# The last stage's matmuls with all wide steps first, and the attention phase's result stores on ScalarE's queue

## The chip, the core and the metric

One core of a Trainium2 chip runs the whole program. The engines that matter are TensorE (PE, matmuls and their weight loads), VectorE (DVE), ScalarE (ACT) and SyncE (SP, which issues DMAs and computes nothing). Each runs its own list of instructions in order and waits on semaphores for the others. A DMA is put on a queue by the engine that issues it, SP or ACT, and is then carried out beside all else. The metric is the device time of one execution in microseconds, the median of the runs.

## What is computed

A memory attention over 8 batches, 8 heads, 576 positions and 64 dimensions, then two MLPs without residuals over the 4608 tokens, each with 512 model dimensions, 2048 hidden ones and a squared ReLU:

```python
a = softmax(phi, axis=2)                       # over 32 memories
k_m = einsum('bhsm,bhsd->bhmd', a, k);  v_m = einsum('bhsm,bhsd->bhmd', a, v)
attn = softmax(q @ k_m.T / 8)
x = (attn @ v_m)  -> (4608, 512)
x = (s * relu(x @ w_in) ** 2 + b) @ w_out      # moe
out = relu(x @ w_in2) ** 2 @ w_out2            # moe2
```

## The kernel before

Every product keeps single-precision accuracy by splitting each operand into a rounded high part and the rest (a "low" part), and adding three products (high x high, high x low, low x high). The last three products also use a scheme with 7 instead of 8 half-size products (`e` = 0 to 6), whose operands are sums and differences of quarter blocks.

There are four stages on TensorE. In the attention phase (lines 786 to 810) the attention is folded into the first layer's input weights: for each batch `b`, unit `f` of 128 hidden columns and half `half` of the 576 positions, `hidden` (line 582) runs 6 matmuls of 288 columns into one of three PSUM banks `hps`, and ACT evicts the bank with a ReLU into half of an SBUF tile `r` (line 593). A tile `r` (five of them) holds both halves, and after the second it is stored to the DRAM tensor `rd`, at line 803. There are 256 such halves and 128 stores. Between them, at slots given by tables, run all the other steps of the phase: transposes (`qps`, `pp`), scores (`sp`), sums (`kvs`), folds (`vps`, evicted by ACT and DVE into `vp`), exponentials, loads of the next batches, and near the end the combination of the first output weights (`wo`, `ws` into `w`) and the first squares and casts of the next stage.

The second stage multiplies the squared `r` by the first output weights (banks `ya`, `yb`, `yc`, 384 columns), the third by the second input weights (banks `pa`, `pb`, `pc`, 384 columns). The last stage (lines 1128 to 1143) takes 18 blocks of 256 tokens; for each of the 7 products of a block, `run` (line 1132) goes over the 8 units `u`. For each it runs one matmul of 512 columns, with the high part of the activations as the stationary operand against the high and low parts of the weights, and one of 256 columns, with the low part of the activations against the high part of the weights. All 16 add into one PSUM bank (`qa`, `qb` or `qc`, picked by `chain` at line 829), the 256-column ones into its first half.

The order of the instructions on ACT, DVE, PE and SP in the attention phase and in the last stage is that of the program text: the wrapper `Written` (line 163; lines 176 and 178 are where every such instruction is recorded) issues each one behind the one before on its engine. In the last stage, ACT's rounding casts (`hi`), DVE's subtractions that make the low parts (`lo`), ACT's evictions (`left`) and DVE's additions (`out`) stand in two lists that `go_on` walks through; before a product it goes on until that product's low part has been issued.

Of the kernel before, what the change touches and what calls it, by code (L numbers as in the profile page):

```python
# [89 lines left out]
def memory_attention_then_two_relu2_mlps(  # L90
# [36 lines left out]
    NU = NF // 2  # L127
# [18 lines left out]
    rd = [[dram.tile([P, NU, S], F32, name=f"rd{b}_{h}") for h in range(2)] for b in range(B)]  # L146
# [35 lines left out]
    pe, act, dve, sp = [Written(e) for e in (nc.tensor, nc.scalar, nc.vector, nc.sync)]  # L182
# [132 lines left out]
    def in_turn(jobs):  # L315
        for job in jobs:
            yield from job
# [52 lines left out]
    weight = lambda key, u, e: w2[key, u, e // 4][:, e % 4]  # L370
# [211 lines left out]
    def hidden(b, f, half, r):  # L582
        pt = at["pt", b]
        hps = ps_h.tile([P, 512], F32, tag="h", name="hps")
        t0 = half * HB
        i = 0
        for hp in range(2):
            w = at["vp", b, f // 4][:, hp, :, (f % 4) * P:(f % 4) * P + P]
            for wi, xi in split3:
                pe.matmul(hps[:, :HB], lhsT=w[:, wi], rhs=pt[xi][:, hp, t0:t0 + HB],  # L590
                                 start=(i == 0), stop=(i == 5))
                i += 1
        st["act"] = act.activation(r[:, t0:t0 + HB], hps[:, :HB], AF.Relu)
# [44 lines left out]
    def wo1_combos(u):  # L638
        tiles = unit_tiles(u)
        for i, t in enumerate(tiles):  # L640
            w2["one", u, i] = t.bitcast(F32R)
        yield from combos(of_out(wo1.pop(u)), lambda: w2["one", u, 0], lambda: w2["one", u, 1])
# [143 lines left out]
    for slot in range(SB * B):  # L786
        b, h = divmod(slot, SB)
        f, half = divmod(h, 2)
        if h == 0 and b == B - 2:
            kpart.close()  # L790
            wpools.append(ctx.enter_context(tc.tile_pool(name="wa", bufs=1)))
            turns.append((in_turn([wo1_combos(u) for u in range(NA)]), 1))
        for go, args in events.pop(slot, []):
            go(*args)
        if h == 0 and b == B - 1:
            lpart.close()
            wpools.append(ctx.enter_context(tc.tile_pool(name="wb", bufs=1)))
            turns.append((in_turn([wo1_combos(u) for u in range(NA, NU)]), 1))
        if half == 0:
            r = r_p.tile([P, S], F32, tag="r", name="r")  # L800
        hidden(b, f, half, r)
        if half == 1:
            sp.dma_start(rd[b][f // NU][:, f % NU], r)
        for turn in turns[:]:
            for _ in range(2):
                if next(turn[0], turns) is turns and turn in turns:
                    turns.remove(turn)
        for go, *args in [x for a, x in zip(BEGUN, BEGIN1) if a == slot]:
            dict(sq=square, cast=cast)[go](0, *args)
# [19 lines left out]
    def chain(e, banks, n, run, name):  # L829


        key = "acacaba"[e]
        start = e in (0, 1, 5)
        if start:
            banks[key] = bank(name + key)
        to = banks[key][:, :n]
        run(to, start)
        return to
# [24 lines left out]
    for n in range(NBLK1):  # L863
        banks, outs = {}, {}
        for e in range(7):
# [5 lines left out]
            start = e in (0, 1, 5)  # L871
            if start:
                banks[key] = [bank("y" + key)[:, :TP] for _ in range(2)]
            to = banks[key]
            for part in range(4):
                for go, *args in parts.pop(28 * n + 4 * e + part, []) + win.pop(28 * n + 4 * e + part, []):
                    go(*args)
                for d in range(2):
                    for u in range(UQ):
                        w = weight("one", part * UQ + u, e)  # L880
                        for i, (wi, xi) in enumerate(split3):
                            pe.matmul(to[d], lhsT=w[:, wi, d], rhs=cast1[n, e, part][:, u, xi],
                                             start=(start and part == 0 and u == 0 and i == 0),
                                             stop=(part == 3 and u == UQ - 1 and i == 2), skip_group_check=True)
# [49 lines left out]
    raws, casts, late = {}, {}, []  # L934
# [41 lines left out]
    for p in range(NPAIR):  # L976
        last = p == NPAIR - 1
        for u0 in range(0, NU, 2):
# [13 lines left out]
            for e in range(7):  # L992
                for u, banked, room in zip(units, banks, rooms):

                    def run(to, start):
                        w, xc = weight("in", u, e), xcs[p, e]
                        for n, (kk, (wi, xi)) in enumerate((kk, s) for kk in range(2) for s in split3):
                            pe.matmul(to, lhsT=w[:, wi, kk], rhs=xc[:, xi, kk],
                                             start=(start and n == 0), stop=(n == 5), skip_group_check=True)
                    to = chain(e, banked, TP, run, "p")  # L1000
                    c11, c12, c21, c22 = [room[:, i, j] for i in range(2) for j in range(2)]
                    out_ = (c11, c22, c12, c12, c22, c11, c21)[e]
                    if e < 3:
                        st["act"] = act.copy(out_, to)
                    elif e < 6:
                        add(out_, to, out_)
                        st["dve"] = dve.scalar_tensor_tensor(out=out_, in0=out_, scalar=0.0, in1=out_,
                                                                   op0=ALU.max, op1=ALU.mult)
                    else:
                        act.activation(out_, to, AF.Relu)  # L1010
                        st["act"] = act.activation(out_, out_, AF.Square)
                    if e > 4:
                        h = e - 5
                        late.append((gd[p][h][:, :, u, :],
                                     room[:, h].rearrange("p t c -> p (t c)").rearrange("p (n c) -> p n c", n=3)))
                        if not (last and u0 == NU - 2):
                            sp.dma_start(*late.pop())
# [104 lines left out]
    def go_on(until):  # L1122
        while not until():
            x = next(x for x in (his, todo) if x and can(*x[0])).pop(0)
            dict(hi=hi, lo=lo, less=less_, out=out_, left=left)[x[0]](*x[1:])
            made.add(x)

    for n in range(NBLK2):
        for e in range(7):
            go_on(lambda: ("lo", e, n) in made and (e not in (2, 3, 4, 6) or ("out", e - 2, n) in made))  # L1130

            def run(to, start):
                for u in range(NU):
                    w = weight("out", u, e).rearrange("p i k c -> p (i k c)")
                    pe.matmul(to, lhsT=casts[n, e](u, 0), rhs=w, start=(start and u == 0), stop=False, skip_group_check=True)
                    pe.matmul(to[:, :256], lhsT=casts[n, e](u, 1), rhs=w[:, :256], start=False, stop=(u == NU - 1),
                              skip_group_check=True)
            banks[n, e] = chain(e, banks, 512, run, "q")
            made.add(("pe", e, n))
            rooms.append(held.pop((n, e)))  # L1140
            if (n, e) == (0, 3):
                rooms += [(rc_turn[0] + i) % 4 for i in range(2)]
# [30 lines left out]
```

## Time and profile before

| what | value |
|---|---|
| median of 3 runs | 1426.86 us (1420.91 to 1429.13) |
| the profiled execution's own time | 1426.42 us |
| its span | 1424.6 us |
| PE busy with matmuls | 1390.2 us (98%) |
| DVE busy | 1118.8 us (79%) |
| ACT busy | 791.3 us (56%) |
| 128 stores `rd` from `r`, issued by SP | 288 KB each, 3.7 us to landing (median) |
| 70 stores of the output from SP, 2 from ACT | 128 KB each, 2.4 and 2.5 us to landing |

Busy times of different engines overlap. A matmul's duration contains its way through the array, so durations of neighbours overlap as well, and the time from one start to the next is what counts. DMA issues are not counted as busy time of an engine, though they hold its queue. Names like `r<-hps` say which tile is written from which; a line number 176 or 178 is that of the wrapper.

### The profile page before, as it was taken

What the parts mean: (1) busy time and instruction counts of PE and PEld (TensorE: products, weight loads), DVE (VectorE), ACT (ScalarE), POOL (GpSimd) and SP (SyncE); (2) the same over time, 40 slices, a digit from 0 to 9 for tenths busy, and PEclk for the clock granted to TensorE, in tenths of its full rate; (3) what the DMA queues carried; (4) which work ended last, traced back from release to release, by engine and by line L of the source; (5) the groups of instructions that cost most, each with busy time, mean ns of one, the idle gap of its engine ahead of it and who ended that gap; (6) DMA issues with size and microseconds to landing.
All of it is one profiled execution on the core that took longest, in us unless ns stands there. A gap on an engine that the chain in (4) does not pass through costs nothing.

```text
span 1424.6 us, 26004 instructions
## 1 busy us (share of the span) xinstructions
PE 1390.2 (98%) x10352; PEld 1293.3 (91%) x10352; DVE 1118.8 (79%) x1670; ACT 791.3 (56%) x1397; POOL 1.2 (0%) x8
## 2 busy tenths in 40 slices
PE   4899999999999999999999999999999999999998
PEld 3788888888999999999999999999998888888887
DVE  6766787676788989898759687686659888888886
ACT  3556666677776877767445455454444444444442
POOL 0000000000000000000000000000000000000000
PEclk9999999999999999999999999999999999999999
DMA  9979889536485674764995664756797434443341
GB/s 308 299 233 302 275 269 293 190 126 216 135 288 164 217 246 152 252 212 165 343 394 191 240 222 174 280 182 257 265 369 268 119 115 140 146 148 119 116 138 35
DMA packets 209160, 306.30 MB, mean 215 GB/s; under 512 B 48400, under 2 KB 163088, under 8 KB 201488
## 3 DMA queue, kind: packets, MB, share of 16 engines
q1 hardware_dynamic: 208880, 304.40, 63.5%
q8 instruction: 81, 1.33, 0.4%
q10 hardware_dynamic: 160, 0.26, 0.1%
q14 instruction: 39, 0.32, 0.1%
HBM read 180.88 MB, written 123.73 MB: 214 GB/s over the span
## 4 chain that ended last, share of the span: by engine, by line
PE 90%; DVE 4%; DMA 2%; ACT 2%; issue 1%; SPq 0%; ACTq 0%; DVEq 0%
PE ya L178 14%; PE qa L178 14%; PE pa L176 13%; PE hps L178 12%; PE yc L178 7%; PE qc L178 7%; PE pc L176 6%; PE yb L178 4%; PE qb L178 3%; PE pb L176 3%; PE vps L178 2%; PE sp L178 1%; DMA gd<-gr 1%; PE kvs L178 1%; PE qps L178 1%
## 5 line engine op out<-in xcount | busy, mean ns | idle before, releaser
L178 PEld LDWEIGHTS hps<-pt,vp 128*128 128x128 f32 x1536 | 210.2, 190 | 36.3 <-issue 18.1
L178 PE MATMUL hps<-pt,vp 128*128 128x288 f32 x1536 | 234.5, 304 | 4.8 <-ACT r L178 2.0
L178 PE MATMUL qa<-w,gc 128*128 128x512 f32 (+1 forms) x1152 | 212.6, 340 | 0.2 <-DVE o L178 0.2
L178 PE MATMUL ya<-rcast,w 128*128 128x384 f32 x1152 | 202.9, 336 | 0.8 <-ACT r L178 0.8
L178 PEld LDWEIGHTS qa<-w,gc 128*128 128x128 f32 x1152 | 176.5, 188 | 27.4 <-DVE o L178 0.5
L178 PEld LDWEIGHTS ya<-rcast,w 128*128 128x128 f32 x1152 | 199.9, 188 | 1.0 <-ACT r L178 1.0
L176 PE MATMUL pa<-xc,w 128*128 128x384 f32 x1056 | 195.3, 337 | 0.0
L176 PEld LDWEIGHTS pa<-xc,w 128*128 128x128 f32 x1056 | 184.5, 188 | 0.5
L178 DVE TENSOR_TENSOR gc<-h,gc 128x1024 fp32r<-128x1024 f32 (+1 forms) x137 | 145.0, 1080 | 23.3 <-ACT gc L178 23.3
L178 ACT CAST gc<-h 128x1024 fp32r<-128x1024 f32 (+1 forms) x137 | 125.1, 938 | 40.1 <-DVE h L178 36.2
L178 ACT ACTIVATE r<-hps 128x288 f32<-128x288 f32 x256 | 104.5, 417 | 66.8 <-PE hps L178 49.8
L178 PE MATMUL qc<-w,gc 128*128 128x512 f32 x576 | 107.7, 340 | 0.0
L178 DVE TENSOR_TENSOR rcast<-r,rcast 128x768 fp32r<-128x768 f32 x96 | 90.6, 954 | 20.9 <-ACT rcast L178 20.1
L178 PE MATMUL yc<-rcast,w 128*128 128x384 f32 x576 | 101.8, 336 | 0.0
L178 PEld LDWEIGHTS qc<-w,gc 128*128 128x128 f32 x576 | 88.2, 188 | 13.5
L178 PEld LDWEIGHTS yc<-rcast,w 128*128 128x128 f32 x576 | 100.0, 188 | 0.0
L176 PE MATMUL pc<-xc,w 128*128 128x384 f32 x528 | 99.6, 336 | 0.0
L178 ACT CAST rcast<-r 128x768 fp32r<-128x768 f32 x96 | 78.2, 834 | 37.9 <-DVE r L178 33.2
L178 ACT COPY o<-qa 128x256 f32<-128x256 f32 x54 | 20.1, 371 | 134.6 <-PE qa L178 134.6
L176 PEld LDWEIGHTS pc<-xc,w 128*128 128x128 f32 x528 | 92.5, 188 | 0.0
L178 DVE TENSOR_TENSOR rcast<-rz,rcast 128x768 fp32r<-128x768 f32 x72 | 68.1, 954 | 16.7 <-ACT rcast L178 16.1
L178 ACT CAST rcast<-rz 128x768 fp32r<-128x768 f32 x72 | 58.7, 836 | 37.8 <-DVE rz L178 24.4
(283 smaller groups left out, 1921.6 us busy)
## 6 DMA issues: line engine op xcount, KB each, us to landing
rd<-r SPq DMA_DIRECT2D x128, 288.0 KB, 3.7
gd<-gr SPq DMA_DIRECT2D x96, 384.0 KB, 3.8
h<-gd SPq DMA_DIRECT2D x34, 1024.0 KB, 4.9
wt<-in_moe_w_out_dram SPq DMA_DIRECT2D x16, 1024.0 KB, 6.6
r<-rd SPq DMA_DIRECT2D x16, 768.0 KB, 5.5
rz<-rd SPq DMA_DIRECT2D x16, 768.0 KB, 5.8
kv<-in_k_dram SPq DMA_DIRECT2D x24, 384.0 KB, 5.3
kv<-in_v_dram SPq DMA_DIRECT2D x24, 384.0 KB, 5.9
```

What stands on the lines that cost most here:

```text
L176: return go(*args, **kwargs)
L178: self.last = go(*args, **kwargs)
```

## The change

Line 803 issues the store of `r` on ACT's queue in place of SP's, right behind the second eviction that it carries away. In the last stage, `run` makes two loops of one: first the 8 matmuls of 512 columns, then the 8 of 256.

```diff
         hidden(b, f, half, r)
         if half == 1:
-            sp.dma_start(rd[b][f // NU][:, f % NU], r)
+            act.dma_start(rd[b][f // NU][:, f % NU], r)
...
             def run(to, start):
+                w = [weight("out", u, e).rearrange("p i k c -> p (i k c)") for u in range(NU)]
                 for u in range(NU):
-                    w = weight("out", u, e).rearrange("p i k c -> p (i k c)")
-                    pe.matmul(to, lhsT=casts[n, e](u, 0), rhs=w, start=(start and u == 0), stop=False, skip_group_check=True)
-                    pe.matmul(to[:, :256], lhsT=casts[n, e](u, 1), rhs=w[:, :256], start=False, stop=(u == NU - 1),
+                    pe.matmul(to, lhsT=casts[n, e](u, 0), rhs=w[u], start=(start and u == 0), stop=False, skip_group_check=True)
+                for u in range(NU):
+                    pe.matmul(to[:, :256], lhsT=casts[n, e](u, 1), rhs=w[u][:, :256], start=False, stop=(u == NU - 1),
                               skip_group_check=True)
             banks[n, e] = chain(e, banks, 512, run, "q")
```

## Rows read from the trace of the kernel before

**Rows 1.** The page's chain that ended last: share of the span by engine

```profile
PE 90%; DVE 4%; DMA 2%; ACT 2%; issue 1%; SPq 0%; ACTq 0%; DVEq 0%
```

**Rows 2.** Busy us by stage; last columns: granted clock, DMA share, GB/s

```profile
0.00:361.00 361.00, 332.26 (x4305) 285.10 (x4306) 258.65 (x463) 225.50 (x545) 1.21 (x8) 0.99 0.77 250
361.00:702.00 341.00, 341.00 (x1968) 341.00 (x1969) 300.70 (x359) 244.50 (x305) 0.00 (x0) 1.00 0.64 213
702.00:1061.00 359.00, 358.14 (x2054) 356.36 (x2052) 257.17 (x449) 169.77 (x329) 0.00 (x0) 1.00 0.71 257
1061.00:1424.00 363.00, 358.80 (x2028) 310.87 (x2028) 302.31 (x402) 151.53 (x219) 0.00 (x0) 1.00 0.44 140
```

The engines stand in the order PE, PEld, DVE, ACT, POOL, each with its count of instructions.

**Rows 3.** The page's groups: busy, mean ns of one | idle before, releaser

```profile
L178 PE MATMUL qa<-w,gc 128*128 128x512 f32 (+1 forms) x1152 | 212.6, 340 | 0.2 <-DVE o L178 0.2
```

**Rows 4.** Timeline (start, us, what): first product, a weight load; loads by form

```profile
1063.49 2.98 PE L178 MATMUL qa<-w,gc 128*128 128x512 f32 x16
...
1056.55 0.32 SPq L178 DMA_DIRECT2D w<-wod  x1
...
w<-wod SPq DMA_DIRECT2D x8, 1024.0 KB, 7.7
```

**Rows 5.** Chain in order of time (start, us, what), 384 and 288 columns

```profile
677.32 8.32 PE yc L178 x48
...
92.74 6.38 PE hps L178 x48
```

**Rows 6.** The same chain in the last stage: two products, one by one

```profile
1106.46 2.82 PE qc L178 x16
1109.28 2.83 PE qa L178 x16
```

**Rows 7.** Groups by form, PE, 1100 to 1424: 512 and 256 columns

```profile
L178 PE MATMUL qa<-w,gc 128*128 128x512 f32 x520 | 186.0, 399 | 0.0
L178 PE MATMUL qa<-w,gc 128*128 128x256 f32 x520 | 146.0, 281 | 0.0
```

**Rows 8.** Groups by form, PE, 361 to 1061: 384 columns

```profile
L178 PE MATMUL yc<-rcast,w 128*128 128x384 f32 x576 | 101.8, 336 | 0.0
```

**Rows 9.** Tile `wsp`: duration ns min/median/max, first and last start

```profile
L178 PEld LDWEIGHTS wsp<-ones,wacc x16: 187/192/192, 290.5 to 292.2; 128*128 128x128 f32 x16
```

**Rows 10.** Tensor `rd`, 40 to 361 us: issues of the stores, ns min/median/max

```profile
L178 SPq DMA_DIRECT2D rd<-r x127: 319/333/1609, 40.6 to 360.8; - x127
```

**Rows 11.** Timeline: an eviction on ACT and its store on SP's queue

```profile
343.48 0.41 ACT L178 ACTIVATE r<-hps 128x288 f32<-128x288 f32 x1
...
343.92 0.32 SPq L178 DMA_DIRECT2D rd<-r  x1
```

**Rows 12.** Timeline, ACT: two evictions back to back

```profile
355.77 0.71 ACT L178 ACTIVATE r<-hps 128x288 f32<-128x288 f32 x2
```

**Rows 13.** Busy us in the attention phase (columns as in rows 2)

```profile
40.00:200.00 160.00, 153.84 (x2282) 128.80 (x2281) 115.93 (x194) 96.00 (x234) 0.00 (x0) 1.00 0.86 272
200.00:331.00 131.00, 131.00 (x1536) 115.15 (x1535) 93.11 (x173) 88.06 (x218) 0.00 (x0) 1.00 0.63 207
331.00:346.00 15.00, 14.45 (x106) 13.89 (x105) 12.04 (x30) 11.81 (x33) 0.00 (x0) 1.00 0.80 264
346.00:361.00 15.00, 12.53 (x84) 11.03 (x83) 10.63 (x21) 14.42 (x32) 0.00 (x0) 1.00 0.61 208
```

**Rows 14.** Tensor `rd`, 331 to 346 and 346 to 361: the stores

```profile
L178 SPq DMA_DIRECT2D rd<-r x9: 319/328/1022, 330.8 to 345.4; - x9
...
L178 SPq DMA_DIRECT2D rd<-r x8: 319/320/455, 346.9 to 360.8; - x8
```

**Rows 15.** Waits, 331 to 361: us in total, times, longest

```profile
PE hps L178 <- ACT r L178: 2.0, 5, 0.9
ACT r L178 <- DMA rd<-r: 1.5, 1, 1.5
```

**Rows 16.** Waits, 40 to 331

```profile
PEld hps L178 <- ACT r L178: 6.7, 8, 0.8
```

**Rows 17.** Tensor `out_dram` from 1380 us on: issues on both queues

```profile
L178 SPq DMA_DIRECT2D out_dram<-o x8: 466/466/590, 1387.5 to 1421.1; - x8
L178 ACTq DMA_DIRECT2D out_dram<-o x2: 497/527/557, 1420.3 to 1421.1; - x2
```

## The prediction

> **What bounds the kernel now.** I read the chain that ended last first, then the busy time of each engine by stage, then single groups of matmuls. TensorE carries 90% of the chain [rows 1], and the table by stage shows the same four times over: the attention phase (0 to 361 us), the two products of the first layer's output (361 to 702), of the second layer's input (702 to 1061) and of its output (1061 to the end) keep PE busy for 332, 341, 358 and 359 us, at a granted clock of 0.99 to 1.00 [rows 2], which is the upper of its two levels, 2.4 GHz. So a change counts if it alters the time from one matmul to the next, or if it makes PE wait. The two edits are in stages with different second-place engines. In the last stage ScalarE (ACT) is busy for 152 of 363 us and nothing presses. In the attention phase ACT is busy for 226 of 361 us [rows 2], and at that phase's end it is already the bound (below).
>
> **The last stage: the order of the wide and the narrow matmuls.** The edit adds and removes no instruction. A product has 8 matmuls of 512 columns and 8 of 256, and there are 18 blocks of 7 products, 126 in all. Before, they alternate; after, 8 wide ones run and then 8 narrow ones. Waits are no source of gain here: PE stood idle for 0.2 us before all 1152 matmuls into the bank `qa` [rows 3]. The new order needs the low halves (`lo`, VectorE) only half a product later, which relaxes a wait that costs nothing now. In the very first product it needs the last weight tile sooner: the eighth wide matmul starts after seven wide ones, not seven pairs. That product starts at 1063.49, and the tile's load is the first part of unit 7, on the queue at 1056.55 with some 7.7 us to landing [rows 4], so at about 1064.3. The new need is at 1063.49 + 7 x 0.227 = 1065.1, so I cost this at nothing; if the load lands as late as others do, it is under 1 us, once.
>
> What remains is the cadence. 48 matmuls of 384 columns take 8.32 us and 48 of 288 columns 6.38 us [rows 5], that is 173.3 and 132.9 ns each. At 2.4 GHz the columns alone are 160 and 120 ns, so a matmul with a weight load of its own costs 13 ns over its columns (13.3 and 12.9), at both widths. A product of the last stage takes 2.825 us [rows 6], or 353 ns for a pair, where columns and twice 13.3 ns make 213.3 + 106.7 + 26.7 = 346.7. Some 6.6 ns of a pair is thus unexplained, 126 x 8 x 6.6 = 6.7 us of the stage. Whether the new order gives it back depends on whose it is. If the narrow matmul's slot is 126.7 ns, because the weights of the next matmul cannot be loaded faster, then eight narrow slots cost the same wherever they stand: change zero. If it comes from changing width at each step, seven of eight such pairs vanish: -5.9 us. From above, a narrow matmul can hardly be slower than the 133 ns of the wider 288: 8 x 6.3 ns more for a product, +6.4 us. From below, 120 ns: -6.7 us.
>
> I take zero, by the mean durations. A 384-column matmul lasts 336 ns, 176 over its columns [rows 8]; a narrow one 281, 174 over them; a wide one 399, 186 over them [rows 7]. The extra 10 ns sits on the matmul that follows a narrow one and whose weights loaded meanwhile. That looks like a wait for weights, which the new order moves and doesn't remove. Against it: 16 weight loads beside two-column matmuls started within 1.7 us, about 113 ns apart [rows 9], so a load alone would fit under 120 ns. I leave that side a fair chance. The Trainium skill (TensorE: Matmul & The Clock Gate, LDWEIGHTS) puts a weight load at its columns over 1.2 GHz, 107 ns for 128, and (Back-to-back issue gap) a matmul at its columns over 2.4 GHz plus 2.5 ns. By both a pair would be 325 ns in either order and the edit would do nothing; the trace's 353 ns shows that the page misses 28 ns of a pair, so it can't decide between the two readings.
>
> **The attention phase: 128 stores move from SP's queue to ACT's.** Each tile `r` is filled by two ACT evictions and then stored. SP issues the store for about 0.33 us (319 to 1609 ns) [rows 10]. It starts right when the second eviction is done: an eviction from 343.48 for 0.41 us, its store at 343.92 [rows 11], 0.03 us later. On ACT the store stands behind that eviction in program order and must wait until its result is written. Everything queued behind it on ACT (the next evictions, casts of `pt` and `vp`, exponentials, the weight casts) waits as well, and PE waits for those through the three `hps` banks.
>
> The price of one store: ACT runs two evictions of 0.41 us in 0.71 [rows 12], so behind an eviction the next instruction starts after 0.30 us. After the change it starts after 0.41 + 0.03 + 0.33 + restart. The trace has no ACT instruction behind a DMA that ACT issued, so the restart is bounded: from 0.04 to 0.15 us, about one to five times the 0.03 us from eviction to store; I take 0.08, the low middle. That is 0.85 - 0.30 = 0.55 us a store.
>
> Where it lands: up to 331 us ACT has room, 64.0 us idle in 40 to 200 and 42.9 in 200 to 331 [rows 13]. 110 stores there would take 60 of 107 us. PE's own weight loads waited for evictions 8 times there, 6.7 us [rows 16]. If each of these spots got one store later, that is 8 x 0.55 = 4.4 us; if none, zero. I take 1.5, nearer to none, since in most of the stretch ACT waits for PE. In 331 to 361 it is different. Here ACT also does casts of weights and the first squares and casts of the next stage, and PE already waits for evictions five times [rows 15]. There are 8 stores in each half from 331 on (17 with the one at 330.8) [rows 14]. ACT's idle time is 15 - 11.81 = 3.2 us in the first half and 15 - 14.42 = 0.6 us in the second [rows 13]. The stores add 8 x 0.55 = 4.4 us to each, so 1.2 and 3.8 us come out over the room, 5.0 us, on the path, since the next stage's first matmul waits for ACT. Together +6.5 us. Low end: 0.50 us a store (4.0 us a half) gives 4.2, less 1.5 us for a wait of ACT for a free `r` tile [rows 15] that an earlier store would shorten: +2.7. High end: ACT's own two stores at the end took 0.53 us each where SP's took 0.47 [rows 17]; with 0.53 and the long restart a store costs 0.82 us, 9.4 at the end and up to 6.6 before: +16.
>
> On SP the 128 stores vanish, with every wait for an eviction in front of the loads behind them. That is worth nothing that I can find: none of the longer waits of PE between 40 and 361 us is for a load, while those for ACT are there [rows 15, 16]. The skill (DMA: Bandwidth & Descriptors, Issuing engines are not separate DMA queues) says that all issuers share the same 16 DMA engines and a second one saves only sequencer time; here it saves SP's, which isn't short, and spends ACT's.
>
> **The sum.** The profiled run took 1426.42 us with a span of 1424.6, beside a median of 1426.86, so it stands for the median within 0.5. 1426.4 + 6.5 + 0 = 1432.9, on the median 1433, +0.4%. A measurement of this kernel can tell about 0.5%, 7.1 us, so this is just inside no change.
>
> **Rivals.**
> Width changes are what costs the 6.6 ns: the last stage gives back 5.9 us and covers the stores, 1427. For it: the 113 ns of loads alone. Against: the 10 ns on the wide ones. Chance 0.28.
> Slower: ACT's queue is held longer than SP's issue shows, by long issues (up to 1609 ns here when DMAs are many [rows 10]) or by a store that waits for an earlier load's semaphore. The place is the whole phase; it decides when a store costs ACT over 107 / 110 = 0.97 us on average before 331, since then ACT is the bound throughout. Already at the high end, 0.82, it is 1426.4 + 16 = 1442; by two thirds of that, 1437 to 1442. Against: the usual issue is 0.33. The skill (Perfetto Trace Analysis, DMA Instruction, HWDGE) has an issue wait for a lock on a shared descriptor generator; with SP and ACT both issuing that would lengthen the store, in this direction. The trace has one such pair, an issue of SP and one of ACT that both began at 1421.1, and neither lasted longer than its queue's others [rows 17], so I give the lock little weight. Chance 0.17.
> The stores cost little, since ACT's end of phase has give that I don't see (the evictions can be late by three banks): 1426.4 + 2.7 or less, 1427 to 1429, and with the first rival 1421. Chance 0.08.
> Narrow after narrow is slower: 1432.9 + 6.4 = 1439. Chance 0.05.
> My own forecast, 1430 to 1436: 0.42.
>
> **How the numbers follow.** Slower by over 0.5% means above 1434.0: the second and fourth rival, and over a third of my own case: 0.17 + 0.05 + 0.16 = 0.38. Faster means below 1419.7, only with both gains at their best: 0.06. The rest, 0.56, is no change. The range is 1423 to 1441: below, the first rival with cheap stores; above, the slower rival short of its end.
>
> **What will show it.** In the last stage: 16 matmuls take 2.825 us (zero), 2.78 (width changes) or 2.88. In the attention phase: DMA issues on ACT, 128 of them, an ACT instruction 0.45 us or so behind each eviction's end, and more matmuls of `hps` that wait for `r` between 331 and the first `ya`, which moves from 360.9 to about 367. If that first `ya` starts before 364, or PE waits are spread from 100 us on, my account of ACT's room is wrong.

## The result and the profile after

| | before | after |
|---|---|---|
| median (range), us, 7 runs each | 1429.01 (1420.91 to 1429.41) | 1435.24 (1432.88 to 1436.26) |
| profiled execution, us | 1426.42 | 1435.44 |
| its span, us | 1424.6 | 1433.6 |
| first matmul of the second stage (`ya`) | 360.88 | 371.99 |
| first matmul of the last stage (`qa`) | 1063.49 | 1074.95 |
| from there to the end of the span | 361.11 | 358.65 |

The ratio is 1.006 with an interval of 1.0043 to 1.0077: slower, with 0.5% inside the interval. Against the 1433.0 that was forecast the median is 2.2 us higher. The table shows that this near hit is made of two misses of opposite sign. The attention phase lost 11.1 us where 6.5 was forecast, the two stages in the middle 0.35, and the last stage gained 2.5 where nothing was forecast: 11.1 + 0.35 - 2.5 = 9.0, the difference of the spans.

The page's chain that ended last, by engine, to set beside [rows 1]:

```profile
PE 87%; DVE 4%; ACT 3%; DMA 3%; SPq 1%; issue 1%; ACTq 1%; DVEq 0%
```

TensorE carries 3 points less than before, and ACT, DMAs and the DMA issues on SP and on ACT 1 point more each. The busy time by stage says where, with the stages cut at their new starts; the columns are those of [rows 2]:

```profile
0.00:372.00 372.00, 339.00 (x4305) 285.81 (x4305) 259.45 (x463) 227.80 (x544) 1.21 (x8) 0.99 0.76 245
372.00:713.00 341.00, 341.00 (x1958) 341.00 (x1959) 300.66 (x358) 244.43 (x304) 0.00 (x0) 0.99 0.63 210
713.00:1072.00 359.00, 358.82 (x2061) 357.69 (x2060) 257.44 (x448) 171.43 (x331) 0.00 (x0) 1.00 0.71 257
1072.00:1433.00 361.00, 355.61 (x2033) 312.22 (x2031) 302.71 (x403) 151.65 (x219) 0.00 (x0) 1.00 0.44 142
```

The two middle stages together are as they were, but not each by itself. The second took 1.6 us more from its first matmul to the third's (351.13 after 349.56), and the third 1.2 less (351.83 after 353.05). Right behind the 1.9 us that PE waited for the first `ya`, the granted clock (last but two) fell from its upper level to the lower one and came back:

```profile
372.00:374.00 2.00, 2.00 (x9) 2.00 (x10) 0.46 (x2) 1.49 (x1) 0.00 (x0) 0.80 0.98 287
374.00:376.00 2.00, 2.00 (x8) 2.00 (x8) 1.62 (x1) 0.35 (x1) 0.00 (x0) 0.50 1.02 310
376.00:378.00 2.00, 2.00 (x11) 2.00 (x10) 1.49 (x2) 2.00 (x3) 0.00 (x0) 0.84 0.99 352
```

Neither edit brings this about each time: behind the same wait the run with batch 7 alone (below) kept 1.00, and its second stage took 349.56 us. So I put the 0.35 down to neither edit.

ACT's busy time in the first stage rose by only 2.3 us (227.80 after 225.50), because an issue doesn't count as busy; the loss is in what stands between ACT's instructions. ACT's timeline shows that (start, us, what, and in brackets the idle time before it with what ended it), once in the quiet case and once in a bad one:

```profile
346.56 0.41 ACT L178 ACTIVATE r<-hps 128x288 f32<-128x288 f32 x1
347.00 0.33 ACTq L178 DMA_DIRECT2D rd<-r  x1
347.37 0.71 ACT L178 CAST w<-wo 128x256 fp32r<-128x256 f32 x2 [0.40 <-ACT r L178]
...
113.80 0.43 ACT L178 ACTIVATE r<-hps 128x288 f32<-128x288 f32 x1
115.76 0.33 ACTq L178 DMA_DIRECT2D rd<-r  x1
116.14 0.52 ACT L178 ACTIVATE x<-x 128x384 f32<-128x384 f32 x1 [1.90 <-DMA kv<-in_v_dram]
```

In the first case the eviction ends at 346.97, the store is issued 0.03 us later for 0.33, and the next instruction starts at 347.37: 0.40 us in which ACT computes nothing. In the second case the eviction ends at 114.23 and the store begins only at 115.76. What ended that wait is the landing of `kv`, a load on SP's queue that this store neither reads nor writes. The trace's semaphore events explain it: the 705 DMAs of the kernel use eight semaphores, 88 or 89 DMAs on each, and of the 697 that have one before them on their semaphore none began before that one had landed. When SP issued the stores, SP alone stood there; now ACT does, with its evictions behind it.

The waits of the matmuls at the end of the phase (341 to 372 here, the stretch that answers to 331 to 361 in [rows 15]): total us, times, longest:

```profile
PEld hps L178 <- ACT r L178: 6.6, 12, 1.2
PE hps L178 <- ACT r L178: 3.7, 9, 0.9
PE ya L178 <- ACT r L178: 1.9, 1, 1.9
```

PE waited there nine times and 3.7 us for evictions, where it had been five times and 2.0 us, and the first `ya` waited 1.9 us for the squares, where it had been 0.8. Earlier on, three stretches of PE (the first two are after, at 117 and 213 us; then the same `vps` matmuls before, at 207 us, in one run of sixteen):

```profile
117.38 0.92 PE L178 MATMUL sp<-kb,qT 128*64 128x64 f32 x24 [1.26 <-ACT qT L178]
212.91 1.09 PE L178 MATMUL vps<-w,vmT 64*32 64x512 f32 x14 [0.38 <-ACT vmT L178]
```

```profile
207.33 1.22 PE L178 MATMUL vps<-w,vmT 64*32 64x512 f32 x16
```

These are waits for ACT that [rows 16] didn't hold: not for evictions, but for the copies `qT` and `vmT`, which stand behind a store in ACT's queue. And in the last stage, single products in the chain (as in [rows 6]), then the groups by form from 1120 us on (as in [rows 7]), then the two places where the last stage waited:

```profile
1121.98 2.79 PE qa L178 x16
1124.77 2.79 PE qc L178 x16
...
L178 PE MATMUL qa<-w,gc 128*128 128x512 f32 x496 | 124.2, 392 | 0.0
L178 PE MATMUL qa<-w,gc 128*128 128x256 f32 x496 | 69.2, 282 | 0.0
...
1077.17 1.09 PE L178 MATMUL qa<-w,gc 128*128 128x512 f32 x6 [0.45 <-DMA w<-wod]
1102.14 1.21 PE L178 MATMUL qa<-w,gc 128*128 128x512 f32 x4 [1.18 <-DVE o L178]
```

A product takes 2.793 us, where it took 2.827: 126 x 0.0334 = 4.2 us back. The matmuls start 226 to 236 ns apart among the wide ones and 113 to 120 ns apart among the narrow ones. At 2.4 GHz the columns of a narrow one are 106.7 ns, so 120 is those and the same 13.3 ns that a 384-column matmul has over its columns, and no more. Against that stand two waits that came once each: the first product took 0.71 us longer (its last weight tile came later than its eighth wide matmul), and around the start of the tenth 1.46 us were lost, 1.18 of them in a wait of PE for VectorE's `o`; the same place had cost 0.42 before. Together -4.2 + 0.7 + 1.5 - 0.4 = -2.4, which is the 2.5 of the table but for rounding.

### The profile page after: what moved, and what is told of

Read it like the earlier page. It is cut to its first block, busy times and chain, and to the rows that moved or that the text cites. A ratio compares the mean times of both kernels' runs of the same rounds, so it can differ in the third digit from the quotient of the medians.

```text
span 1433.6 us, 25932 instructions
## 1 busy us (share of the span) xinstructions
PE 1394.4 (97%) x10352; PEld 1296.7 (90%) x10352; DVE 1120.3 (78%) x1670; ACT 795.3 (55%) x1397; POOL 1.2 (0%) x8
## 3 DMA queue, kind: packets, MB, share of 16 engines
q8 instruction: 81, 1.33, 0.4%
## 4 chain that ended last, share of the span: by engine, by line
PE 87%; DVE 4%; ACT 3%; DMA 3%; SPq 1%; issue 1%; ACTq 1%; DVEq 0%
PE ya L178 14%; PE qa L178 13%; PE pa L176 13%; PE hps L178 10%; PE yc L178 7%; PE qc L178 6%; PE pc L176 6%; PE yb L178 3%; PE qb L178 3%; PE pb L176 3%; PE vps L178 2%; DMA gd<-gr 1%; PE sp L178 1%; PE kvs L178 1%; ACT r L178 1%; SPq L178 1%
## 5 line engine op out<-in xcount | busy, mean ns | idle before, releaser
L178 PEld LDWEIGHTS qa<-w,gc 128*128 128x128 f32 x1152 | 180.9, 190 | 26.3 <-DVE o L178 1.4
L178 PE MATMUL qc<-w,gc 128*128 128x512 f32 (+1 forms) x576 | 106.4, 337 | 0.0
L178 PEld LDWEIGHTS qc<-w,gc 128*128 128x128 f32 x576 | 91.1, 190 | 12.1
```

The costliest lines, as they stand in the source:

```text
L178: self.last = go(*args, **kwargs)
```

## Experiments

Each ratio is against runs of the kernel before that were made beside it. To read where the attention phase loses, I take the starts of its 256 halves of a tile (a half is six `hps` matmuls, 0.8 us; a store follows each second half; batch b is halves 32b to 32b + 31) and subtract those of the kernel before. The start of the first half alone lay up to 0.6 us earlier and 1.2 us later in other executions, so shifts are given from there or within a stretch. Batch 0 can't be read so closely: in kernels that don't issue its stores on ACT it took from 1.1 us less to 1.2 us more than in the profile of before, with granted clocks of 0.66 to 1.00 in single stretches of 10 us up to 70 us.

### The stores alone

```diff
-            sp.dma_start(rd[b][f // NU][:, f % NU], r)
+            act.dma_start(rd[b][f // NU][:, f % NU], r)
```

> The stores on ACT's queue alone, the last stage in the old order. If the two parts add up (in the traces the first matmul of the second stage moved from 360.9 to 372.0 us), this is 11 us slower than before, ratio 1.0078, and slower than the whole change by the 2.4 us that the last stage gave back there. Rival: the first stage's shift is chance of its early loads, which fell differently in that execution; then the loss is 6 us or less, ratio 1.004. Per store I expect ACT's next instruction 0.40 to 0.46 us after the end of the eviction before it.

1435.2 us, ratio 1.0086 (1.0055 to 1.0117), first `ya` at 372.40, products of 2.827 us throughout. So the loss of the phase comes from the stores and not from the new order. By halves the shift grows by 1.0 in batch 0, 3.6 in batches 1 and 2, 2.6 in batches 3 to 6 and 3.1 in batch 7, and by 1.1 more up to `ya`.

### The stores of one part of the phase

Batches 0 to 6, and batch 7 alone:

```diff
-            sp.dma_start(rd[b][f // NU][:, f % NU], r)
+            (act if b < B - 1 else sp).dma_start(rd[b][f // NU][:, f % NU], r)   # and: if b == B - 1
```

> The 112 stores of batches 0 to 6 on ACT, the 16 of batch 7 on SP, old order in the last stage. By the prediction's working, ACT has room up to 331 us and this costs 1.5 us. By the steps between the two traces, it costs 6 to 7 us (ratio 1.0045), some 2 of it at three stores that wait 0.5 to 1.6 us for an earlier load's semaphore.

> Only the 16 stores of batch 7 on ACT, old order in the last stage. By the prediction's working this costs 5.0 us (ratio 1.0035). By the steps between the two traces 3.5 to 4.4 us (ratio 1.003). If it is under 1 us, the end of the phase isn't where ACT's room ends.

Batches 0 to 6: 1429.73 us, ratio 1.0051 (1.003 to 1.0072). Batch 7: 1426.36, ratio 1.0024 (1.0002 to 1.0046). The first `ya` of each:

```profile
369.38 0.62 PE L178 MATMUL ya<-rcast,w 128*128 128x384 f32 x2 [0.81 <-ACT r L178]
```

```profile
366.76 0.61 PE L178 MATMUL ya<-rcast,w 128*128 128x384 f32 x2 [1.87 <-ACT r L178]
```

The wait in brackets sorts the two places. With the end's stores on SP it is 0.81 us as before; with them on ACT it is 1.87 as in the changed kernel. `ya` comes 8.5 us late with the early stores (7.9 of it by the end of batch 6, and 2.5 of that in batch 0, where the granted clock from 50 to 60 us was 0.66 after 1.00) and 5.9 with the late ones, of which 1.5 was there before the first of these was issued: 4.4 at the end. The early part costs more than the end even without batch 0 (5.4 us in batches 1 to 6), and within their intervals the ratios agree with that of the stores alone: 1.0051 and 1.0024 make 1.0075 beside 1.0086.

### The stores of batches 1 and 2, and of batches 3 to 6

```diff
-            sp.dma_start(rd[b][f // NU][:, f % NU], r)
+            (act if b in (1, 2) else sp).dma_start(rd[b][f // NU][:, f % NU], r)   # and: if 3 <= b <= 6
```

> Only the 32 stores of batches 1 and 2 on ACT, old order in the last stage: the stretch in which three or four stores on ACT waited 0.3 to 2.0 us for an earlier load. Theory one: the loss before the phase's end is mostly these waits, so this loses 3 to 5 us within the two batches, with at least two stores that wait over 0.3 us. Theory two: it is the held queue in every batch alike, 32 of 128 stores, 2 us or less here.

> Only the 64 stores of batches 3 to 6 on ACT, old order in the last stage. No store waited long for a load there in two of three executions. Theory one: 2 to 3 us lost, 1.3 of it at one place near 212 us where PE waits for ACT's copy of vmT. Theory two: 64 of 128 stores, 3.5 to 5 us.

One timed execution each: 1428.68 and 1429.15 us beside 1426.93. The times are too close together to say anything; the shifts are not. They grew, in us, by:

| halves | after | batches 1 and 2 | batches 3 to 6 |
|---|---|---|---|
| 32 to 95 (batches 1 and 2) | 3.9 | 2.6 | 0.0 |
| 96 to 223 (batches 3 to 6) | 2.6 | 0.0 | 4.2 |
| of the latter, at half 123 | 1.29 | 0.0 | 1.31 |

Each part's loss appears where its stores are on ACT and is gone where they are on SP. What is lost is kept: nothing of it is won back behind. Two amounts differ from the changed kernel's. Of the 1.3 us that are missing in batches 1 and 2, 0.76 are half 72 and 0.42 half 33. The step at 72 followed a store that waited 1.6 us for a load in the changed kernel (from 140.26 to 141.84); here no store of batch 2 waited over 0.3. Half 33 comes behind the last store of batch 0, which is on SP here. The store at 115 us waited again, and for the same load, and half 56 again came 1.33 us late, as in the changed kernel. (Neither expectation fits the 2.6 us: they were 3 to 5, and 2 or less.) ACT's timeline of the run with batches 1 and 2:

```profile
115.39 0.33 ACTq L178 DMA_DIRECT2D rd<-r  x1
115.76 0.52 ACT L178 ACTIVATE x<-x 128x384 f32<-128x384 f32 x1 [1.90 <-DMA kv<-in_v_dram]
```

The 1.5 us too many in batches 3 to 6 come from the clock. At half 191 it fell to the lower level, as the windows show (last but two: granted clock), and the shift grew by 1.9 there where it was 0.4 in the changed kernel, which issues the same stores on ACT. Without that 1.5 the loss is 2.7 us, inside the 2 to 3 of the first theory:

```profile
292.00:294.00 2.00, 1.69 (x22) 1.60 (x29) 0.22 (x1) 0.40 (x2) 0.00 (x0) 1.00 0.23 86
294.00:296.00 2.00, 2.00 (x18) 0.46 (x5) 0.00 (x0) 0.34 (x1) 0.00 (x0) 0.52 0.03 8
296.00:298.00 2.00, 2.00 (x26) 1.72 (x27) 1.29 (x2) 1.14 (x3) 0.00 (x0) 0.63 0.00 0
```

### The stores on ACT, but each behind the next tile's first eviction

```diff
+        if half == 0 and kept:
+            act.dma_start(*kept.pop())
         if half == 1:
-            sp.dma_start(rd[b][f // NU][:, f % NU], r)
+            kept.append((rd[b][f // NU][:, f % NU], r))
```

(and one more for the last tile.)

> All stores on ACT, but each one behind the first eviction of the next tile, so that its own tile has long been written when ACT comes to it; old order in the last stage. Theory one: a store costs ACT some 0.5 us because it waits for the end of the eviction just before it; then the issue now runs beside the next eviction, the next ACT instruction starts 0.05 to 0.15 us late in place of 0.5, and the first matmul of the second stage comes at 362 to 365 us, the time at most 1.003 of before. Theory two: the loss is the issue itself, the waits for earlier loads' semaphores or the second queue's traffic; then that first matmul stays at 369 to 373 us, ratio 1.006 to 1.009.

1432.27 us, ratio 1.0061 (1.0039 to 1.0084); the profiled execution took 1424.84. The ten times fall in two groups, three up to 1427.4 and seven from 1432.1, and the profile is in the lower one. `ya` at 366.17, so the phase lost 5.3 us, not 11, between the two theories. ACT's timeline, one store late in the phase and the worst one early on:

```profile
333.41 0.41 ACT L178 ACTIVATE r<-hps 128x288 f32<-128x288 f32 x1 [0.38 <-PE hps L178]
333.41 0.33 ACTq L178 DMA_DIRECT2D rd<-r  x1
333.78 0.48 ACT L178 CAST pt<-pp 128x384 fp32r<-128x384 f32 x1
...
140.22 0.41 ACT L178 ACTIVATE r<-hps 128x288 f32<-128x288 f32 x1 [0.38 <-PE hps L178]
143.00 0.33 ACTq L178 DMA_DIRECT2D rd<-r  x1
143.37 1.07 ACT L178 CAST vp<-vps 128x512 fp32r<-128x512 f32 x2 [2.73 <-DMA wt<-in_moe_w_out_dram]
```

At 333.41 the issue lies inside the eviction, and the cast behind it starts 0.37 us after the eviction's start, where 0.30 is usual without a store [rows 12]. In the 30 places where an instruction stood ready like this, it was 0.37 to 0.44. So an issue whose data were finished one instruction earlier costs ACT 0.07 to 0.13 us, as the first theory had it, and nothing where ACT waits for PE anyway. From half 96 to the last half nothing was lost (-0.4 us). So most of the 0.55 us that was forecast for a store is paid because the issue must wait for the eviction just ahead of it. What is left is the other term, and the clock behind it. Between halves 64 and 96 the shift grew by 3.5 us. One store waited 2.4 us there for the semaphore of `wt`, a weight that it has nothing to do with, and half 72 came 2.0 us late. Behind that wait the granted clock fell, and halves 73 to 75 lost 1.4 us more:

```profile
144.00:146.00 2.00, 1.80 (x7) 1.56 (x8) 1.28 (x2) 1.58 (x4) 0.00 (x0) 0.68 0.82 245
146.00:148.00 2.00, 2.00 (x10) 2.00 (x9) 0.91 (x1) 1.35 (x3) 0.00 (x0) 0.50 0.59 188
```

Another store waited 0.9 us at 112.54, and no half came later for it. The remaining 1.75 us of the phase are batch 0's.

### The stores from GpSimd

```diff
-            sp.dma_start(rd[b][f // NU][:, f % NU], r)
+            nc.gpsimd.dma_start(rd[b][f // NU][:, f % NU], r)
```

> All stores issued by GpSimd, which has nothing else to do, old order in the last stage. If the loss is ACT's held queue, the attention phase takes what it took before, the second stage starting at 360 to 363 us, ratio 0.998 to 1.002. If it is that stores on a second queue disturb the loads on SP's, or that SP's loads come in another order, the second stage starts at 368 us or later here as well, ratio 1.006.

1420.8 us, ratio 0.9992 (0.9967 to 1.0017). The issues (ns min/median/max) and the first `ya`:

```profile
L803 POOL DMA_DIRECT2D rd<-r x128: 542/542/707, 37.5 to 361.4; - x128
361.07 0.79 PE L178 MATMUL ya<-rcast,w 128*128 128x384 f32 x3 [0.81 <-ACT r L178]
```

The issues are 0.2 us longer each than ACT's, and `ya` starts at 361.07, among the profiles with all stores on SP (359.7 to 362.8). From batch 1 to the end of batch 6 the shift changes by 0.0 us, where the stores on ACT made it grow by 6.6. GpSimd has hardly anything else to do (1.2 us busy before). So a second queue and its traffic cost nothing that these rows show; what costs is that ACT is held. The run also shows that SP's freed queue is worth nothing: the loads behind the stores no longer wait for evictions here, and PE is not earlier. The Trainium skill (DMA: Bandwidth & Descriptors, Issuing engines are not separate DMA queues) says a second issuer saves only sequencer time; this run agrees.

### The order of the last stage alone

```diff
+                w = [weight("out", u, e).rearrange("p i k c -> p (i k c)") for u in range(NU)]
                 for u in range(NU):
-                    w = weight("out", u, e).rearrange("p i k c -> p (i k c)")
...
+                for u in range(NU):
```

> The new order of the last stage alone, the stores on SP. Theory one: a product takes 2.793 us in place of 2.827, as in the changed kernel, 126 x 0.034 = 4.2 us, and the two single waits that stood beside it there (0.7 us for the last weight tile, 1.3 us for a VectorE addition) stay: 2.3 us faster, ratio 0.998. Theory two: the waits came from the shifted stores and go: 4.2 us faster, ratio 0.997. Rival from the prediction: the order is worth nothing, ratio 1.000.

1422.53 us (1420.64 to 1424.84), ratio 0.9988 (0.9972 to 1.0005). Products of 2.793 us as in the changed kernel, no wait in the first product, and 0.72 us lost ahead of the tenth. The order does give 0.033 us a product back against the profile of before, yet the time hardly moves. The runs of the kernel before beside it are why: of 30, 20 lie under 1424.6 and 10 from 1426.2 to 1428.8. The wide order has one group. The next run looks at the lower group of before.

### The kernel before, once more

> The kernel before, once more. In the runs with the late stores on ACT a product of the last stage took 2.83 us until a wait in the ninth product and 2.773 us from there to the end, in the old order. If the old order has two cadences, and which one holds is decided by how PE's last wait ended, this execution has one or the other from the ninth or tenth product on: 2.83 or 2.773 us, and nothing between; with 2.773 it should be near 1420, with 2.83 near 1427. If the cadence belongs to the program, it is 2.83 again.

1418.88 us, 7.5 less than the profiled execution of [rows 1 to 17], with a first `ya` at 360.49, 0.4 earlier. The chain in the last stage, product by product, from the ninth on:

```profile
1085.32 2.83 PE qc L178 x16
1088.15 2.82 PE qa L178 x16
1090.97 2.77 PE qc L178 x16
1093.75 2.77 PE qa L178 x16
```

The same instructions in the same order run at two cadences. From the eleventh product on this execution takes 2.773 us and not 2.827, and it stays there to the end: 116 x 0.0534 = 6.2 us, about the distance of the two groups. A pair's two starts lie 230 + 117 ns apart at 2.773, and in a pattern of three steps (241 + 120, 236 + 114, 232 + 118) at 2.827. Of the profiles with the old order, four changed to 2.773 at this very place (this one, batch 7 alone, the delayed stores, GpSimd), and the other five (before, stores alone, batches 0 to 6, 1 and 2, 3 to 6) stayed at 2.827; where a kernel's times fall in two groups, its profiled execution lies in the group that its cadence names.

Just ahead of it a weight load is late. The loads (PEld) of the ninth, tenth and eleventh product in this run:

```profile
1085.05 2.77 PEld L178 LDWEIGHTS qc<-w,gc 128*128 128x128 f32 x16
1087.93 2.73 PEld L178 LDWEIGHTS qa<-w,gc 128*128 128x128 f32 x16
1090.70 2.73 PEld L178 LDWEIGHTS qc<-w,gc 128*128 128x128 f32 x16
```

From the ninth to the tenth product the loads step by 2.88 us, then by 2.77. The matmuls of the tenth were not late for it. In three of the four that changed (this one, the delayed stores, GpSimd) it went so, with no time lost on PE. In the other six profiles PE itself lost 0.14 to 0.52 us at the tenth product, and of these one changed cadence (batch 7 alone, 0.52) and five did not.

### Two more orders

Products 2, 4 and 6 of a block of seven (counted from 0) with the narrow eight first, so that most products begin at the width at which the one before ended; and, in another kernel, wide, narrow, narrow, wide for each two units:

```diff
+                kinds = (1, 0) if e in (2, 4, 6) else (0, 1)      # narrow first in these products
...
+                    for i in (1, 0) if u % 2 else (0, 1):         # the other kernel
```

> Stores on SP. In the last stage products 0, 1, 3, 5 wide first, products 2, 4, 6 narrow first, so that a block of 7 products goes from narrow to wide 4 times in place of 7. If what is left over 2.773 us in the wide-first order (0.020 us a product) is the price of each step from narrow to wide, a block takes 19.49 us in place of 19.55, 1.1 us in all; if it is anything else that a product has once, 19.55 or more.

> The order of e8 again, timed. With 2.785 us a product in every execution it should lie at 1420 to 1422 without the second group of times that the kernel before has near 1427: a ratio of 0.996 to 1.000, and a spread as small as that of the wide-first order alone (4 us).

> Stores on SP. In the last stage a unit's wide matmul comes first in even units and its narrow one first in odd units, so that widths run W N N W W N N W and a product goes from narrow to wide 4 times. If each such step costs the 0.020 us that it costs behind eight narrow ones, a product takes 2.773 + 0.080 = 2.853 us, slower than the old order; if the price needs a long run of narrow ones, 2.773 to 2.80 us, and the time is 0.996 to 1.000 of before. As in the old order, there may be two cadences.

The first: 1421.09 in one execution, then 1422.2 (1420.19 to 1424.36, leaving out one of 1470.11, which lost 50.5 us in its second stage, where the order is the same), ratio 0.9981 (0.9957 to 1.0005), a product of 2.785 us in the mean. The second: 1422.7 (1420.67 to 1424.49), ratio 0.9977 (0.9957 to 0.9996), a product of 2.787. One group of times each. The first's 7 x 2.785 = 19.49 us a block is what the price of a step from narrow to wide would give, but the second, with four such steps in a product, isn't at 2.853. The chain of the first, then of the second:

```profile
1128.06 2.80 PE qa L178 x16
1130.86 2.77 PE qc L178 x16
1133.63 2.80 PE qa L178 x16
```

```profile
1126.89 2.79 PE qc L178 x16
1129.67 2.79 PE qa L178 x16
```

Over the best of 2.773, the products are longer by 20 ns (wide first), 13 (pairs), 11 (narrow first in three of seven, a mean) and 53 (the old order's worse cadence), that is by 3, 2, some 1.7 and 8 times 6.67 ns. The number of width changes doesn't order them: pairs change width eight times in a product and cost less than wide first with its two. In the kernel with narrow first in three of seven, a wide run behind a wide run keeps 227 ns throughout and one behind eight narrow matmuls starts at 233 to 236: in these orders the extra time stands behind runs of narrow ones. All three orders are steady, and none of them is faster than the old order at its better cadence.

## Why the prediction came out as it did

**The price of a store: right.** 0.55 us was forecast, with 0.44 from the eviction's end to the next instruction. Where ACT had its next instruction ready, the rows show 0.40 to 0.47, with 0.326 us of issue (0.394 at most) and 0.04 to 0.10 of restart, so 0.51 to 0.58. "An ACT instruction 0.45 us or so behind each eviction's end" held, but for the stores that waited for loads.

**The end of the phase: right in kind, a little high in size.** 5.0 us forecast; 4.3 in the changed kernel, 4.4 with batch 7 alone. The reading by ACT's idle time carries it. The two halves of that stretch now are:

```profile
341.00:356.50 15.50, 14.53 (x98) 13.03 (x97) 12.35 (x28) 11.93 (x34) 0.00 (x0) 1.00 0.64 204
356.50:372.00 15.50, 10.82 (x67) 8.89 (x66) 8.88 (x17) 12.87 (x27) 0.00 (x0) 1.00 0.65 215
```

In the second one ACT is idle for 15.5 - 12.87 = 2.6 us, and that is six pauses of 0.40 to 0.46 us, each between an eviction and what stands behind its store: nothing else is left, ACT is the bound.

**Before 331 us: the step that failed.** "I take 1.5, nearer to none, since in most of the stretch ACT waits for PE." The halves show 6.8 us by the end of batch 6, 7.3 counted from the phase's start. Of these 0.7 are batch 0's, which can be chance; 6.6 came in batches 1 to 6, beyond the 4.4 that I had as eight known waits and as much as the high end. The sign that I had named for it came too: waits of PE from 117 us on. Two things were wrong with it.

First, the room was averaged. ACT had 107 us of it in 291, but not where it counts. Before, around the `vps` matmuls that moved the halves behind them by 1.3 us in each kernel with these stores on ACT behind their evictions:

```profile
202.50:208.50 6.00, 6.00 (x56) 4.99 (x54) 3.81 (x10) 5.81 (x17) 0.00 (x0) 1.00 1.01 330
```

ACT is busy for 5.81 of these 6 us and the copy `vmT`, which sixteen matmuls need, is the last but a few in the row. Three stores in that stretch put 1.3 us ahead of it, and PE was not waiting there before, so a count of the places where it already waited [rows 16] couldn't find it. Cut into pieces of 5 us, the stretch from 200 on has eight in which ACT is busy for over 4.0; five of them hold a step of 0.18 us or more, and of the six such steps of batches 3 to 6 only the one at half 191 lies elsewhere. Those six make 2.5 us, and like ones in batches 1 and 2 (halves 33, 64, 84, 95) 1.6.

Second, the wait for an earlier load's semaphore stood among my rivals and not in the sum. It cost 1.33 us at half 56 and 0.76 at half 72, 2.1 us together, and in the run with delayed stores it is the one term that is still seen. How long it lasts differs from execution to execution: the store at 115 us met it in all four profiles that issue it there (1.5 us here, 2.0 with the stores alone, 0.4 with batches 0 to 6, 1.5 with batches 1 and 2), other stores in some.

**The last stage: zero was wrong, and so was the reason.** I held that the 10 ns on a wide matmul were a wait for weights that a narrow one is too short to cover. The narrow matmuls follow one another at 120 ns, their columns and the usual 13.3 ns, so the weight loads fit; the side that I left "a fair chance", 113 ns between two loads, was the right one. The 10 ns aren't even the order's: in the kernel before once more, at 2.773 us a product, the wide matmuls last 391 ns and not 399:

```profile
L178 PE MATMUL qa<-w,gc 128*128 128x512 f32 x464 | 162.8, 391 | 0.0
```

And the 6.6 ns of a pair that the sum left unexplained are the distance of the two cadences, 353.3 and 346.7. The rival, -5.9 us, is nearer in size (-4.2 from the cadence), but its cause falls too: the old order has the width change at each step and runs at 2.773 us when it changes cadence, below the new order. What I took as the price of a structure was one of two cadences of the same instruction stream; a single profile can't show that. Against the better one the wide order costs 116 x 0.020 = 2.3 us. What sets the cadence stays open. It changes only at the tenth product, where a weight load is late; it did so in the three profiles in which PE lost nothing there, and in one of six in which it did. How far a product's first weight load runs ahead of its first matmul doesn't tell the cadences apart (114 ns at the better one; 110, 115 and 118 in turn at the other), and no kernel here set it on purpose.

**The first product and the tenth.** "I cost this at nothing; if the load lands as late as others do, it is under 1 us, once": 0.71 us, once. The loss at the tenth product, 1.46 us where it was 0.42, I didn't foresee: I took the 0.2 us that PE idled for `o` [rows 3] as a sign that nothing presses there.

**The other rivals.** A lock between the issuing queues isn't seen: ACT's longest issue is 0.394 us (in the run with delayed stores one of 128 took 0.86). "ACT is the bound throughout" didn't come about either: a store cost ACT 0.63 us in the worst batch's mean, not 0.97. Narrow after narrow is not slower.

**What the errors made together.** +4.6 us in the attention phase, -2.5 in the last stage, +0.35 between: 2.5 us over the 1432.9 of the sum. The time is right for reasons of which half are wrong, and luck is in the comparison too. Of the seven runs of the kernel before beside the changed one, six lie in its upper group, 1426.9 to 1429.4; of the thirty beside the first experiments, twenty lie in the lower. Against the median of those thirty, 1423.15, the same 1435.24 would be 0.85% slower (an estimate, since these weren't run side by side). The gain of 2.5 us in the last stage is likewise one against the worse cadence: from the first `qa` on, the kernel before once more took 354.53 us, less than the 358.65 of the changed one.

**The best version.** The stores left on SP and the narrow and wide matmuls in pairs (0.9977), wide first (0.9988), or the stores on GpSimd (0.9992): medians from 1420.8 to 1422.7, of which only the first has an interval that ends below 1, and that beside runs of before of which 11 of 19 were in its upper group. None is shown to beat the kernel before at its better cadence, 1418 to 1424.6 us.

## What to carry to other kernels

The DMAs issued from a compute engine here cost it the wait for its own last result and for whatever the DMA's semaphore still held, not only the issue; one instruction more between the result and the store brought 0.55 us down to 0.13 or less, and an idle engine's queue took all of it off. Room on an engine is to be read in the dense stretches and by what hangs on the last instruction of each, never from an average, and not only where something waits already. Before a cadence is explained, look whether the same instructions run at it in a second profile.

## What was not expected of the hardware

- TensorE runs one stream of alternating 512- and 256-column matmuls with weight loads of their own at two stable cadences, 346.7 or 353.3 ns a pair, and changes from one to the other in mid-stage. The steady products of all orders differ by multiples of 6.67 ns.
- 256-column matmuls with a new 128-column weight load each follow one another at 120 ns, 13.3 ns over their columns, as the 384-column ones do at 173.3.
- An issue on ACT lies beside the eviction that runs there, if it doesn't depend on it (both at 333.41).
- The granted clock fell to its lower level behind short waits of PE in single executions, and each time cost more than a microsecond: behind 0.32 us at 293.8 us (batches 3 to 6; 1.5 us), behind 1.9 us at 372 us (the changed kernel; 1.6 us) and behind 1.8 us at 144 us (delayed stores; 1.4 us). The changed kernel idled 0.31 us at the first of these places, and the run with batch 7 alone 1.87 us at the second, and both kept 1.00.
